# First row tiles through two PSUM tiles, earlier Sqrt table, other order of the first loads

## The chip, the cores and the metric

The kernel runs on one core of one Trainium2 chip. The metric is the device time of one execution in microseconds (us); lower is better.

PE is the matmul engine, PEld its weight loads, DVE is VectorE, ACT is ScalarE, POOL is GpSimd, SP is SyncE; ACTq and SPq are DMA issues on those engines' queues. Times in a trace count from the start of its span.

## The reference

An attention branch over 2048 rows of width 640 (32 heads of 192, the last 512 keys), a gated hidden layer (SwiGLU), and a gate that joins them. What matters here is the start of the second:

```
xn = (x - mean(x)) / sqrt(var(x) + 1e-5)          # per row, x: 2048 x 640
B  = (silu(xn @ w_gate) * (xn @ w_up)) @ w_down   # w_gate, w_up: 640 x 1536
out = x + attention(xn) * silu(B)
```

## The kernel before

The hidden layer is computed first, in four blocks of 512 rows. The first block can't wait for everything to be loaded, so it is cut into four row tiles of 128 rows. Each is normalised (statistics on DVE, the root on ACT, the scaling on DVE), transposed on PE in five chunks of 128 columns into PSUM, copied to SBUF (`xnT`), and multiplied with the first 384 columns of both weight matrices. A weight chunk is the 128 rows of a matrix that meet one of the five chunks of `xnT`; gate and up chunks are those of w_gate and w_up. Chunk-major order takes chunk by chunk over all six sums, bank-major order sum by sum over all five chunks. These make three pairs of hidden columns, f = 0, 1, 2, for which six PSUM banks stay open over the four tiles. After that come f = 3 to 11 with 512 rows at a time.

```python
        load_x(0)
        load_x(1, nc.scalar)
        for cs in (slice(0, 1), slice(1, 3), slice(3, NC)):      # weight chunks 0, 1-2, 3-4
            if cs.stop == NC:
                load_x(2)
            for eng, w_sb, w in ((nc.sync, wg_sb, B_w_gate), (nc.scalar, wu_sb, B_w_up)):
                ...
                eng.dma_start(out=w_sb[:, cs, 0:FQ], in_=src)
        load_x(3)
        ...
        nc.scalar.activation(act_t[:], one_t[:], ACT.Sqrt)       # brings in the table
        warm = sc_tile()
        keep_warm(11)                                            # dummy matmuls
        ...
        def ready(t):
            ln_transpose(t)                                      # five, all into one PSUM tile
            rows = slice(t * P, (t + 1) * P)
            n = NC if t else 2
            nc.scalar.copy(xnT[:, 0:n, rows], tps[t][:, 0:n, :])
            if n < NC:
                nc.vector.tensor_copy(out=xnT[:, n:NC, rows], in_=tps[t][:, n:NC, :])

        ln_stats(0)
        ln_sqrt(0)
        ln_stats(1, lambda: ln_apply(0, (slice(0, 2 * P), slice(2 * P, D))))
        ready(0)
        ln_sqrt(1)
        keep_warm(3)
        ...
        for t in range(4):
            order = [(*fs, [c]) for c in range(NC) for fs in banks]     # chunk-major
            if t:
                order = [(*fs, range(NC)) for fs in banks]              # bank-major
            for k, (f, s, cs) in enumerate(order):
                if k == len(order) * 3 // 5 and t < 3:
                    if t == 1:
                        ln_stats(3, lambda: ln_apply(2))
                    else:
                        ln_apply(t + 1)
                    ready(t + 1)
                    ...
                hidden_mm(first[f][s][:, rows], s, f, rows, cs)
        ...
        for b in range(NB):
            for f in range(NF):
                ...
                if b or f >= 3:
                    ffn_hidden(b, f)          # 10 matmuls, then Silu on ACT and the product on DVE
                if nx and 1 <= f < 5:
                    ln_stats(4 * b + 3 + f)   # statistics of the next block's rows, on DVE
```

The softmax here doesn't subtract the row's maximum and nothing guards it: scores larger than these inputs give would overflow.

## Time and profile before

| | before |
|---|---|
| time, median of 3 runs | 925.96 us (925.85 to 926.03) |
| span of the trace | 924.2 us |
| PE busy | 916.6 us |
| first real matmul | 7.01 us |
| transposes of row tiles 0, 1, 2, 3 start | 5.90, 8.53, 10.63, 12.75 us |
| first 512-column matmul (f = 3) | 15.65 us |
| f = 6 starts | 22.13 us |

The prediction below shows the page, the busy times by stretch and the start of the timeline. One more view also belongs here, which it did not look at: DVE after the row tiles, with the Silu table load on ACT before it and the start of f = 6 on PE (timeline; start, length, engine, line, operation, and in brackets the idle time before and what ended it).

### The profile page before, as it was taken

How to read it: one execution, taken by the hardware profiler on the slowest of the kernel's cores; microseconds unless marked ns; L12 is line 12 of the kernel's file. 1: busy time of each engine (PE TensorE's matmuls, PEld its weight loads, DVE VectorE, ACT ScalarE, POOL GpSimd, SP SyncE). 2: the span in 40 equal slices, each digit the busy share in tenths (PEclk: the TensorE clock that was granted, in tenths of full speed). 3: DMA queues.
4: the chain of work that ended last, by engine and by line, in shares of the span. 5: the costliest groups of instructions: out<-in, count | busy, mean ns of one | idle time of the engine just before them, and what ended most of it. 6: DMA issues, size and time to landing. Idle time of an engine off the chain costs nothing.

```text
span 924.2 us, 25783 instructions
## 1 busy us (share of the span) xinstructions
PE 916.6 (99%) x11101; PEld 622.6 (67%) x11101; DVE 576.1 (62%) x844; ACT 473.8 (51%) x847; POOL 100.1 (11%) x387
## 2 busy tenths in 40 slices
PE   9999999999999999999999999999999999999997
PEld 5455555575858585868686767676767777776665
DVE  6433331467676767676666667676767676767655
ACT  4222223546464656555556465655555555656561
POOL 0000000000000000000000000000000000002977
PEclk9999999999999999999999999999999999999999
DMA  9321510044544443444636252635371717162624
GB/s 297 74 54 35 114 35 1 1 81 86 83 83 80 86 80 86 72 94 66 100 59 107 57 109 53 112 50 116 45 121 40 126 37 129 35 132 74 145 47 140
DMA packets 243810, 77.18 MB, mean 84 GB/s; under 512 B 224624, under 2 KB 243696, under 8 KB 243696
## 3 DMA queue, kind: packets, MB, share of 16 engines
q1 hardware_dynamic: 242640, 74.72, 40.7%
q8 instruction: 87, 1.43, 0.7%
q10 hardware_dynamic: 1056, 0.82, 0.3%
q14 instruction: 27, 0.22, 0.1%
HBM read 39.45 MB, written 2.62 MB: 46 GB/s over the span
## 4 chain that ended last, share of the span: by engine, by line
PE 98%; DMA 1%; DVE 1%; ACTq 0%; issue 0%; ACT 0%; DVEq 0%
PE mm L430 22%; PE sc L565 19%; PE sc L444 18%; PE mm L470 16%; PE sc L276 11%; PE mm L298 6%; PE sc L539 3%; PE mm L522 2%; PE mm L539 1%; DMA wu_sb<-in_B_w_up_dram 1%; PE mm L276 0%; PE mm L311 0%; PE sc L522 0%; PE sc L470 0%; PE mm L444 0%
## 5 line engine op out<-in xcount | busy, mean ns | idle before, releaser
L448 ACT ACTIVATE p_t<-sc 128x1024 bf16<-128x1024 f32 x254 | 253.0, 1022 | 128.9 <-PE sc L444 128.9
L435 DVE TENSOR_REDUCE qT<-mm 128x512 bf16<-128x1024 f32 x189 | 230.9, 1223 | 91.6 <-PE mm L430 89.2
L500 ACT ACTIVATE O_b<-mm,r 128x192 bf16<-128x192 f32 x486 | 164.6, 421 | 183.6 <-issue 162.4
L430 PE MATMUL mm<-xnT,wq_p 64*128 64x512 bf16 x1890 | 240.0, 376 | 0.0
L590 DVE TENSOR_TENSOR sacc<-sacc,sc 128x640 f32<-128x640 f32 x200 | 164.2, 821 | 89.5 <-PE sc L565 89.5
L565 PE MATMUL sc<-wo_p,OT_b 64*128 64x320 bf16 x2592 | 217.0, 296 | 0.0
L444 PE MATMUL sc<-qT,khat 64*128 64x512 bf16 x1524 | 198.1, 376 | 0.5 <-DVE sacc L588 0.5
L470 PE MATMUL mm<-V_p,p_t 64*128 64x193 bf16 x3520 | 186.2, 242 | 0.1
L470 PEld LDWEIGHTS <-p_t 64*128 64x128 bf16 x3584 | 162.4, 93 | 12.9 <-issue 0.6
L430 PEld LDWEIGHTS <-wq_p 64*128 64x128 bf16 x1890 | 104.7, 94 | 95.7 <-issue 0.5
L565 PEld LDWEIGHTS <-OT_b 64*128 64x128 bf16 x2592 | 139.4, 94 | 22.2
L444 PEld LDWEIGHTS <-khat 64*128 64x128 bf16 x1536 | 85.1, 94 | 80.1 <-issue 0.7
L553 POOL MEMSET turn_t<- 128x1 f32 x328 | 32.2, 98 | 697.0 <-PE mm L470 474.6
L284 DVE TENSOR_TENSOR hT<-sc,sg 128x512 bf16<-128x512 f32 x46 | 31.7, 690 | 85.2 <-ACT sg L283 85.1
L283 ACT ACTIVATE sg<-sc 128x512 bf16<-128x512 f32 x46 | 27.3, 596 | 72.4 <-PE sc L276 72.4
L276 PE MATMUL sc<-xnT,wu_sb 128*128 128x512 bf16 (+1 forms) x260 | 59.1, 354 | 0.2 <-DMA wu_sb<-in_B_w_up_dram 0.2
L276 PE MATMUL sc<-xnT,wg_sb 128*128 128x512 bf16 (+1 forms) x260 | 59.2, 354 | 0.1
L298 PE MATMUL mm<-wd_sb,hT 128*128 128x320 bf16 x384 | 56.6, 299 | 0.0
L489 DVE RECIPROCAL r<-mm 128x4 f32<-128x4 f32 x124 | 22.7, 183 | 47.8 <-PE mm L470 36.3
L298 PEld LDWEIGHTS <-hT 128*128 128x128 bf16 x384 | 37.6, 98 | 18.9
L276 PEld LDWEIGHTS <-wu_sb 128*128 128x128 bf16 x285 | 26.3, 98 | 27.2 <-DMA wu_sb<-in_B_w_up_dram 0.4
L276 PEld LDWEIGHTS <-wg_sb 128*128 128x128 bf16 x285 | 26.4, 98 | 23.1 <-issue 0.2
(68 smaller groups left out, 372.9 us busy)
## 6 DMA issues: line engine op xcount, KB each, us to landing
wo_p<-in_A_wo_dram SPq DMA_DIRECT2D x16, 480.0 KB, 4.2
K_p<-in_A_k_cache_dram SPq DMA_DIRECT2D x32, 192.0 KB, 3.3
V_p<-in_A_v_cache_dram SPq DMA_DIRECT2D x32, 192.0 KB, 3.1
wq_p<-in_A_wq_dram SPq DMA_DIRECT2D x64, 80.0 KB, 3.2
wq_p<-in_A_wq_dram SPq DMA_DIRECT2D x16, 160.0 KB, 3.4
x_r<-in_A_x_dram SPq DMA_DIRECT2D x16, 160.0 KB, 3.9
x_t<-in_A_x_dram SPq DMA_DIRECT2D x14, 160.0 KB, 3.0
OT_b<-O_b SPq DMA_TRANSPOSE x124, 2.8
```

The source lines that it names most:

```text
L276: nc.tensor.matmul(out, w_sb[:, c, f * P : (f + 1) * P], xnT[:, c, qc], start=(c == 0), stop=(c == NC - 1),)
L298: nc.tensor.matmul(dn[:, 0:HD], hTs[b][:, f, ti * P : (ti + 1) * P], wd_sb[:, f, cols], start=(f == 0), stop=(f == NF - 1),)
L430: nc.tensor.matmul(q_ps[:, h, :], pairs[pr]["wq"][r, c, j * P : (j + 1) * P], xnT[r, c, b * 512 : (b + 1) * 512], start=(c == 0), stop=(c ...
L435: nc.vector.reduce_sum(qTs[i][:, j, :], q_ps[:, :, :].rearrange("p h n -> p n h"), axis=AX.X)
L444: nc.tensor.matmul(sc[:, h, :], khat[r, j, ks], qT[r, j, :], start=(j == 0), stop=(j == 2))
L448: nc.scalar.activation(p_t[:, :, :], sc[:, :, :], ACT.Exp, scale=scale)
L470: m = nc.tensor.matmul(acc[:, k, h * 256 : h * 256 + Dh + 1], Ps[i][kc][r, h, qt * P : (qt + 1) * P], V_p[r, kc, h, 0 : Dh + 1], start=(p ...
L500: nc.scalar.activation(O_b[:, qt, h, :], a_k[:, h, 0:Dh], ACT.Copy, scale=r[:, k, h, :])
L539: nc.tensor.matmul(ps, OTs[i][:, 3 * qt + j, :], pairs[i // NB]["wo"][:, j, n * HD : (n + 1) * HD], start=(first and j == 0), stop=(end an ...
L553: st["turn"] = nc.gpsimd.memset(turn_t[:], 0.0)
L565: m = nc.tensor.matmul(ps[:, n, 0:HD], OTs[i][r, 3 * qt + j, :], pairs[i // NB]["wo"][r, j, n * HD : (n + 1) * HD], start=(turn == 0 and j ...
L590: nc.vector.tensor_tensor(s_t, s_t, sc[:, :, 0:HD], ALU.add)
```

## The change

It means to bring the first real matmuls forward: the Sqrt table is loaded while the first transfers run, the first two chunks of a row tile go to a PSUM tile of their own so that their copy need not wait for all five transposes, ACT makes both copies, and x tile 2 goes behind weight chunk 3. Tiles 1 and 2 run chunk-major to suit this. The PSUM banks of the start belong to a pool that is closed after f = 3.

```diff
@@ loads
-        for cs in (slice(0, 1), slice(1, 3), slice(3, NC)):
-            if cs.stop == NC:
-                load_x(2)
-            for eng, w_sb, w in ((nc.sync, wg_sb, B_w_gate), (nc.scalar, wu_sb, B_w_up)):
-                ...
+        load_first(slice(0, 1), (nc.sync, nc.sync))       # gate on the first engine, up on the second
+        load_first(slice(1, 3), (nc.sync, nc.sync))
+        nc.scalar.activation(act_t[:], one_t[:], ACT.Sqrt)
+        load_first(slice(3, 4), (nc.sync, nc.scalar))
+        load_x(2)
+        load_first(slice(4, NC), (nc.sync, nc.scalar))
         load_x(3)
@@ PSUM, dummies
-        nc.scalar.activation(act_t[:], one_t[:], ACT.Sqrt)
-        keep_warm(11)
+        PARTS = (slice(0, 2), slice(2, NC))
+        tps = [psum1.tile([P, 8, P], bf, name="tp", tag="tp%d" % n) for n in range(2)]
+        ...
+        keep_warm(9)
+        keep_warm(6, P)
@@ ready(t)
-            n = NC if t else 2
-            nc.scalar.copy(xnT[:, 0:n, rows], tps[t][:, 0:n, :])
-            if n < NC:
-                nc.vector.tensor_copy(out=xnT[:, n:NC, rows], in_=tps[t][:, n:NC, :])
+            for tp, cs in zip(tps, PARTS):
+                for k, c in enumerate(range(cs.start, cs.stop)):
+                    nc.tensor.transpose(tp[:, k, :], xn[:, c * P : (c + 1) * P], ident[:])
+            for tp, cs in zip(tps, PARTS):
+                nc.scalar.copy(xnT[:, cs, rows], tp[:, 0 : cs.stop - cs.start, :])
@@ row tiles
-        keep_warm(3)
-            if t:
+            if t == 3:
                 order = [(*fs, range(NC)) for fs in banks]
@@ after the row tiles
+        ffn_hidden(0, 3, [psum1.tile([P, 512], f32, name="gu3", tag="tp%d" % n)[:, :] for n in range(2)])
+        early.close()
+        mm_pool.append(...)
-                if b or f >= 3:
+                if b or f >= 4:
                     ffn_hidden(b, f)
```

More of the change, by code (lines that the diff above doesn't have):

```diff
@@ L68 @@
     qpool = ctx.enter_context(tc.tile_pool(name="att_q", bufs=2))
-    psum = ctx.enter_context(tc.tile_pool(name="psum", bufs=2, space=bass.MemoryType.PSUM))
+    sc_pool = ctx.enter_context(tc.tile_pool(name="psum_sc", bufs=2, space=bass.MemoryType.PSUM))
+    mm_pool = []
     def sc_tile():
-        return psum.tile([P, 2, 512], f32, name="sc", tag="sc")
+        return sc_pool.tile([P, 2, 512], f32, name="sc")
     def mm_tile():
-        return psum.tile([P, 2, 512], f32, name="mm", tag="mm")
+        return mm_pool[0].tile([P, 2, 512], f32, name="mm")
     ctx.enter_context(tc.manual_schedule())
@@ L181, in load_x, with load_first @@
             x_t[t] = lnx.tile([P, D], bf, name="x_t")
-            if t == 0:
-                for r, eng in ((lo, nc.sync), (hi, nc.scalar)):
-                    eng.dma_start(out=x_t[t][r, :], in_=x2[t * P + r.start : t * P + r.stop, :])
-            else:
-                eng.dma_start(out=x_t[t][:], in_=x2[t * P : (t + 1) * P, :])
+            for r, eng in ((lo, nc.sync), (hi, nc.scalar)) if t == 0 else ((slice(0, P), eng),):
+                eng.dma_start(out=x_t[t][r, :], in_=x2[t * P + r.start : t * P + r.stop, :])
+        def load_first(cs, engs):
+            for eng, w_sb, w in zip(engs, (wg_sb, wu_sb), (B_w_gate, B_w_up)):
+                src = w[cs.start * P : cs.stop * P, 0:FQ].rearrange("(c p) f -> p c f", p=P)
+                eng.dma_start(out=w_sb[:, cs, 0:FQ], in_=src)
         def load_gu(q):
@@ L198 @@
         load_x(1, nc.scalar)
-        for cs in (slice(0, 1), slice(1, 3), slice(3, NC)):
-            if cs.stop == NC:
-                load_x(2)
-            for eng, w_sb, w in ((nc.sync, wg_sb, B_w_gate), (nc.scalar, wu_sb, B_w_up)):
-                src = w[cs.start * P : cs.stop * P, 0:FQ].rearrange("(c p) f -> p c f", p=P)
-                eng.dma_start(out=w_sb[:, cs, 0:FQ], in_=src)
+        load_first(slice(0, 1), (nc.sync, nc.sync))
[4 more added lines that the diff above has]
+        load_first(slice(4, NC), (nc.sync, nc.scalar))
         load_x(3)
@@ L211, with keep_warm @@
         nc.sync.dma_start(out=wd_sb[:], in_=B_w_down.rearrange("(f p) d -> p f d", p=P))
-        nc.scalar.activation(act_t[:], one_t[:], ACT.Sqrt)
-        warm = sc_tile()
-        def keep_warm(n):
-            for _ in range(n):
-                nc.tensor.matmul(warm[:, 0, :], zero_t[:, 0:P], zero_t[:], start=True, stop=True)
-        keep_warm(11)
+        early = ExitStack()
+        psum1 = early.enter_context(tc.tile_pool(name="psum1", bufs=1, space=bass.MemoryType.PSUM))
+        PARTS = (slice(0, 2), slice(2, NC))
+        tps = [psum1.tile([P, 8, P], bf, name="tp", tag="tp%d" % n) for n in range(2)]
+        first = [
+            [gu[:, s, :] for s in range(2)]
+            for gu in (sc_tile(), sc_tile(), psum1.tile([P, 2, 512], f32, name="gu"))
+        ]
+        def keep_warm(n, cols=512):
+            for _ in range(n):
+                nc.tensor.matmul(
+                    first[2][1][:, 0:cols], zero_t[:, 0:P], zero_t[:, 0:cols], start=True, stop=True
+                )
+        keep_warm(9)
+        keep_warm(6, P)
         def ln_stats(t, between=None):
@@ L256, in ln_apply @@
                 )
-        tps = {}
-        def ln_transpose(t):
-            xn = xns.pop(t)
-            tps[t] = tp[:, t % 2, 0 : NC * P].rearrange("p (c k) -> p c k", c=NC)
-            for c in range(NC):
-                nc.tensor.transpose(tps[t][:, c, :], xn[:, c * P : (c + 1) * P], ident[:])
         def ln_transpose_dma(t):
@@ L284, in hidden_gate, with ffn_hidden @@
             nc.vector.tensor_tensor(hTs[b][:, f, :], u, sg[:], ALU.mult)
-        def ffn_hidden(b, f):
-            gu = mm_tile() if (b, f) == (0, 3) else sc_tile()
+        def ffn_hidden(b, f, gu=None):
+            gu = gu or [sc[:, s, :] for sc in (sc_tile(),) for s in range(2)]
             for s in range(2):
-                hidden_mm(gu[:, s, :], s, f, slice(b * 512, (b + 1) * 512))
-            hidden_gate(b, f, gu[:, 0, :], gu[:, 1, :])
+                hidden_mm(gu[s], s, f, slice(b * 512, (b + 1) * 512))
+            hidden_gate(b, f, *gu)
         def ffn_down(b, u):
@@ L317 @@
         hTs[0] = ffh.tile([P, NF, 512], bf, name="hT")
-        first = {f: [sc[:, s, :] for s in range(2)] for f, sc in ((0, sc_tile()), (1, sc_tile()))}
-        tp = psum.tile([P, 2, 1024], bf, name="tp", tag="mm")
-        first[2] = [mm[:, s, :] for mm in (mm_tile(),) for s in range(2)]
         def ready(t):
-            ln_transpose(t)
-            rows = slice(t * P, (t + 1) * P)
-            n = NC if t else 2
-            nc.scalar.copy(xnT[:, 0:n, rows], tps[t][:, 0:n, :])
-            if n < NC:
-                nc.vector.tensor_copy(out=xnT[:, n:NC, rows], in_=tps[t][:, n:NC, :])
+            xn, rows = xns.pop(t), slice(t * P, (t + 1) * P)
+            for tp, cs in zip(tps, PARTS):
[3 more added lines that the diff above has]
+                nc.scalar.copy(xnT[:, cs, rows], tp[:, 0 : cs.stop - cs.start, :])
         ln_stats(0)
@@ L359 @@
                     hidden_gate(0, f, *first[f])
+        ffn_hidden(0, 3, [psum1.tile([P, 512], f32, name="gu3", tag="tp%d" % n)[:, :] for n in range(2)])
+        early.close()
+        mm_pool.append(ctx.enter_context(tc.tile_pool(name="psum_mm", bufs=2, space=bass.MemoryType.PSUM)))
         nc.gpsimd.memset(V_p[:, :, :, Dh : Dh + 2], 1.0)
```

## The prediction

> **What bounds the kernel now.** I read the page first: its busy shares, its digits in 40 slices and its chain of waits.
>
> ```profile
> PE 916.6 (99%) x11101; PEld 622.6 (67%) x11101; DVE 576.1 (62%) x844; ACT 473.8 (51%) x847; POOL 100.1 (11%) x387
> ...
> DMA  9321510044544443444636252635371717162624
> ...
> PE 98%; DMA 1%; DVE 1%; ACTq 0%; issue 0%; ACT 0%; DVEq 0%
> ```
>
> The matmul engine is the bound: of the 924.2 us span it is busy 916.6, and the chain that ended last runs 98% through it. Only 7.6 us are left in which it does nothing. The transfers show 9 in the first slice alone. So I asked for busy time by stretch, to see where those 7.6 us lie (columns: stretch, length, busy us of PE, PEld, DVE, ACT, POOL with counts, clock, DMA share, GB/s).
>
> ```profile
> 0.00:15.60 15.60, 13.56 (x154) 9.62 (x155) 7.42 (x25) 6.34 (x13) 0.79 (x8) 1.00 0.89 273
> 15.60:176.00 160.40, 160.40 (x925) 86.55 (x924) 56.68 (x109) 49.31 (x89) 3.81 (x6) 1.00 0.26 61
> 176.00:185.00 9.00, 9.00 (x86) 4.09 (x84) 6.92 (x8) 6.03 (x6) 0.00 (x0) 1.00 0.01 2
> 185.00:895.00 710.00, 709.37 (x9750) 503.99 (x9745) 487.54 (x678) 406.56 (x724) 75.98 (x360) 1.00 0.44 83
> 895.00:924.20 29.20, 24.28 (x199) 18.39 (x196) 17.50 (x27) 5.53 (x16) 19.56 (x13) 0.98 0.49 136
> ```
>
> From 15.6 to 895 us PE is full, less 0.6 us. The change touches nothing after about 17 us: with line and buffer numbers left out, the two programs' instruction orders are the same from there on, except that one set of PSUM banks is handed over earlier. So what it can win is what it takes off the start, before PE becomes full. Every us by which the 4 row tiles of the first block finish sooner should reach the end, because nothing later waits for anything but PE.
>
> The timeline of that start (start, length, engine, line, operation, and in brackets the idle time before it and its releaser):
>
> ```profile
> 3.57 0.89 DVE L229 BATCH_NORM_STATS2 stats<-x_t 128x6 f32<-128x320 bf16 x2 [2.40 <-DMA x_t<-in_A_x_dram]
> 3.58 1.28 ACT L214 ACT_TABLE_LOAD   x1 [3.58 <-DMA x_t<-in_A_x_dram]
> ...
> 4.87 0.20 ACT L214 ACTIVATE act_t<-one_t 128x1 f32<-128x1 f32 x1
> ...
> 4.98 0.28 ACT L242 ACTIVATE rstd<-mv,eps_t 128x1 f32<-128x1 f32 x1
> ...
> 6.56 0.37 ACT L327 COPY xnT<-tp 128x256 bf16<-128x256 bf16 x1 [1.30 <-PE tp L264]
> ...
> 6.97 0.36 DVE L329 COPY xnT<-tp 128x384 bf16<-128x384 bf16 x1 [0.19 <-ACT xnT L327]
> ...
> 7.91 0.23 PE L276 MATMUL sc<-xnT,wu_sb 128*128 128x128 bf16 x1 [0.24 <-DMA wu_sb<-in_B_w_up_dram]
> ...
> 9.31 0.49 DVE L229 BATCH_NORM_STATS2 stats<-x_t 128x6 f32<-128x320 bf16 x1 [0.40 <-DMA x_t<-in_A_x_dram]
> ```
>
> The reader should see three kinds of wait: a table load stuck behind a DMA issue, so the first Sqrt starts at 4.98 although its statistics end at 4.70; a copy at 6.56 that waits for all five transposes, and a second that waits for the first; and two transfers that are themselves late, the weight chunk at 7.91 and x tile 3 at 9.31.
>
> **What the Trainium skill says.** "ScalarE: Activation LUTs", section "What ACT_TABLE_LOAD costs", gives about 1283 ns for a load plus about 1380 ns for a drain. The trace has 1.28 us for the load, with the next activation right behind it, so I count 1.28 us, no drain. "PSUM — Partial Sum Buffer", section "PSUM bank collisions raise a hardware error", says accesses of two engines must be kept apart by bank and quadrant, two readers included. The trace agrees: the DVE copy starts 0.03 us after the ACT copy of the same bank ends. "DMA: Bandwidth & Descriptors", section "Issuing engines are not separate DMA queues", says that spreading issues over engines saves only issue time. The trace fits: both queues together move 330 to 350 GB/s from 5.4 us on. "TensorE: Matmul & The Clock Gate", section "What's actually happening", puts the cold array at half clock until a busy window has passed; here the dummy matmuls go from 427 ns apart to 216 at 4.61 us.
>
> **The change part by part.**
>
> *Table load.* ACT now does it after two issues, about 1.9 to 3.4 us, hidden. The statistics end at 4.70; the Sqrt can start near 4.74 instead of 4.98. The reciprocal then waits for the statistics half in front of it (4.62 + 0.44 = 5.06) and starts near 5.09 instead of 5.29: **0.20 us** off the chain to the first transpose, 5.90 to about 5.69. The 9 + 6 dummy matmuls fit before it: they end near 5.2 if the clock rises at 4.61 again.
>
> *Two PSUM tiles.* The first copy waits only for two transposes. In the trace the second transpose starts at 5.96 and takes 0.22, against 6.54 for the last: some 0.33 us earlier. It starts near 6.02, ends near 6.39, and PE's first real matmul comes at 6.44 instead of 7.01. The same trace has a further 0.11 us hole at 7.12 to 7.23, where the third real matmul waits for the dummies that wrote its tile; the dummies now write another tile. So the first chunk's six matmuls end **0.65 to 0.7 us** earlier, at about 6.78.
>
> *Both copies on ScalarE.* A copy costs 0.372 us for 256 columns and 0.692 for 640, thus 0.83 ns a column; 384 cost about 0.48. Both, overlapping by 0.09, take 0.76 in place of 0.69: later row tiles get their last chunks 0.1 later but their first two some 0.25 sooner, which suits the new chunk-major order of tiles 1 and 2. DVE is spared 0.36 us once.
>
> *Chunk-major order.* In tiles 1 and 2, 12 matmuls instead of 15 follow the next tile's transposes: 12 x 56 ns = 0.67 us instead of 0.84. PE then stood 0.16 to 0.26 us at the head of each of tiles 1 to 3 for the five-chunk copy. Together about 0.2 us a tile, if the next tile is ready.
>
> *Transfers.* All arrive at the same saturated engines. Before, up chunk 1-2 (ACT queue) landed at 7.86 while gate chunk 1-2 had landed at 6.95, x tile 2 at 7.70, last weights at 8.64 and 8.82, x tile 3 at 9.29. Ahead of the second weight chunk there are now about 0.92 MB and no x tile 2 (0.16 MB), which at 330 GB/s is 0.5 us: I estimate it at 7.0 to 7.3. x tile 2 slides by perhaps 0.3 us to 8.0; x tile 3 has the same 1.64 MB through it, so 8.8 to 9.3.
>
> *The sum.* Now go along the row tiles. Tile 0 starts at 6.44, runs dry at 6.78 and waits for the second weight chunk to about 7.1; tile 1's transposes come near 7.85 instead of 8.53, tile 1 starts near 8.9 instead of 9.76, 0.8 us ahead. Then tile 2 meets the transfers. In DVE's order the statistics of x tile 3 come before tile 2 is normalised, so tile 2's transposes come no earlier than x tile 3's landing plus 1.25 us (0.49 + 0.16 + 0.45 and the gaps between), or x tile 2's plus 2.35. With 9.1 and 8.0 that is 10.35, against 10.63. Of the 0.8 us only about 0.3 survives there. Tile 3's transposes follow 2.1 us later, as before (2.12), because that distance is a chain of DVE and ACT and not of PE; then the 0.15 to 0.2 us of the order comes on top. End of the block: 0.3 + 0.15, about **0.45 us** sooner, and the rest of the kernel moves along with it. 925.96 - 0.45 = 925.5.
>
> **The rivals.** *First: the transfers take it all.* If x tile 3 lands at 9.3 or later again, tile 2 is not earlier, and only the shorter tail of each tile is left: 0.15 to 0.2 us, time 925.8. For it: the DMA engines were at their ceiling and the bytes are the same; x tile 2 even goes later, and issuing x tile 3 now has to wait for an up chunk to land. Against: the following large weight transfer is also issued later and competes less with it. *Second: the transfers get better than I think.* With fewer descriptors in front, both x tiles could land 0.5 us earlier; then the 0.8 us of tile 1 survives: 925.1. *Third: ScalarE becomes the bound of the start.* It carries two copies, Sqrt and two issues per tile; but 0.76 + 0.30 in a period of 2.1 us leaves half of it free. *Fourth: the hidden start.* If the clock of the array rises later than 4.61 us, 15 shorter dummies with no later refill leave it cold at the first tile: 30 matmuls at 107 ns instead of 56 would cost up to 1.5 us. The trace shows full clock from 4.61, so I give this little. *Fifth: the new PSUM layout or handover delays the second block.* Its banks are free long before; nothing.
>
> **Range and chances.** Three runs of before differ by 0.2 us, so the noise is small; the size of the gain is the doubt. From no gain (first rival with a bit of bad luck) to 1.0 us (second) gives 924.95 to 925.95. Over 2% would be 18.5 us; the whole start with idle PE is 2 us, so 2% faster can't happen, and 2% slower would take a fault I don't see.
>
> **What would show each step.** Right: the table load at about 2 us and the first Sqrt near 4.75; first transpose near 5.7; first copy near 6.0, while later transposes still run; first real matmul near 6.45; a wait for a weight chunk until about 7.1; first 512-column matmul after the row tiles near 15.2 instead of 15.65; after that equal durations and no new wait. Wrong: the first real matmul not before 6.8; tile 2's transposes at 10.6 or later, or before 10.0; the weight chunk later than 7.5; or a gain at the start that is gone again at the end.

## More of the kernel before

From f = 4 on, two PSUM tiles take turns for the hidden columns (f = 3 has another one): f = 6 writes the tile that f = 4 used, and may only do so when DVE has formed f = 4's product.

```profile
13.95 1.28 ACT L356 ACT_TABLE_LOAD   x1
...
15.96 1.29 DVE L284 TENSOR_TENSOR hT<-sc,sg 128x512 bf16<-128x512 f32 x2 [3.27 <-ACT sg L283]
17.16 0.68 DVE L284 TENSOR_TENSOR hT<-mm,sg 128x512 bf16<-128x512 f32 x1
17.76 0.88 DVE L229 BATCH_NORM_STATS2 stats<-x_t 128x6 f32<-128x320 bf16 x2
...
19.79 0.64 DVE L284 TENSOR_TENSOR hT<-mm,sg 128x512 bf16<-128x512 f32 x1
20.35 0.88 DVE L229 BATCH_NORM_STATS2 stats<-x_t 128x6 f32<-128x320 bf16 x2
...
21.38 0.64 DVE L284 TENSOR_TENSOR hT<-sc,sg 128x512 bf16<-128x512 f32 x1
...
22.13 1.24 PE L276 MATMUL sc<-xnT,wg_sb 128*128 128x512 bf16 x5
```

From its first product at 15.96 DVE has no waiting row in this stretch: the bracket stands only on the first. It does products and statistics back to back, and f = 4's product (the last DVE row) ends at 22.02. PE takes up f = 6 at 22.13. In the changed kernel PE follows such a product by 0.055 us when it really waits for it, so PE could have started at 22.08 here. It came 0.05 us later than it was allowed to. No wait is shown, and there is almost no room either.

## The result, and the profile after

The changed kernel takes 925.76 us (median of 6 runs, 925.57 to 925.99), the kernel before 925.90 us in 6 runs (925.52 to 926.17). The ratio is 0.9999 with a 95% interval of 0.9986 to 1.0011: the same. A ratio here is the mean time of one kernel's fast runs over that of the other's of the same rounds, so it is not quite the ratio of the medians.

| | before | changed | predicted |
|---|---|---|---|
| first transpose | 5.90 | 5.63 | 5.69 |
| first real matmul | 7.01 | 6.37 | 6.44 |
| second gate chunk / up chunk lands | 6.95 / 7.86 | 7.31 / 7.71 | - / 7.0 to 7.3 |
| x tile 2 / x tile 3 lands | 7.70 / 9.29 | 8.43 / 9.07 | 8.0 / 8.8 to 9.3 |
| transposes of tile 1 | 8.53 | 8.38 | 7.85 |
| transposes of tile 2 | 10.63 | 10.64 | 10.35 |
| first 512-column matmul | 15.65 | 15.34 | 15.2 |
| f = 6 starts | 22.13 | 22.09 | with the lead of the row before |

A landing is the start of an issue plus the time to landing that the trace gives for it. The page's busy shares and chain of the changed kernel:

```profile
PE 916.3 (99%) x11102; PEld 627.2 (68%) x11102; DVE 575.8 (62%) x843; ACT 474.4 (51%) x851; POOL 100.1 (11%) x387
...
PE 97%; DVE 1%; DMA 0%; SPq 0%; issue 0%; DVEq 0%
```

Nothing has moved that a page could show. The timeline of the start answers to the rows in the prediction:

```profile
1.94 1.28 ACT L204 ACT_TABLE_LOAD   x1 [1.94 <-issue]
2.00 0.38 ACTq L189 DMA_DIRECT2D wu_sb<-in_B_w_up_dram  x1
...
4.70 0.29 ACT L254 ACTIVATE rstd<-mv,eps_t 128x1 f32<-128x1 f32 x1 [1.26 <-DVE mv L244]
...
5.95 0.82 ACT L331 COPY xnT<-tp 128x256 bf16<-128x256 bf16 x2 [0.96 <-PE tp L329]
...
7.35 0.23 PE L280 MATMUL sc<-xnT,wg_sb 128*128 128x128 bf16 x1 [0.48 <-DMA wg_sb<-in_B_w_gate_dram]
...
7.76 0.23 PE L280 MATMUL sc<-xnT,wu_sb 128*128 128x128 bf16 x1 [0.18 <-DMA wu_sb<-in_B_w_up_dram]
...
8.45 0.89 DVE L241 BATCH_NORM_STATS2 stats<-x_t 128x6 f32<-128x320 bf16 x2 [0.81 <-DMA x_t<-in_A_x_dram]
```

The Sqrt now waits for its statistics and not for the table, and the copies start at 5.95 instead of 6.56. But after six real matmuls PE stands still for the gate chunk and then for the up chunk, and DVE for x tile 2. Where before one matmul waited 0.24 us for a weight chunk, now two wait, 0.66 us in all. The second row shows something else: the issue of up chunk 3 goes out at 2.00 while the table load runs (1.94 to 3.22).

And ACT, DVE and PE after the row tiles, in the same timeline:

```profile
13.74 1.28 ACT L357 ACT_TABLE_LOAD   x1
...
15.76 1.29 DVE L288 TENSOR_TENSOR hT<-sc,sg 128x512 bf16<-128x512 f32 x2 [3.17 <-ACT sg L287]
...
16.96 1.50 DVE L288 TENSOR_TENSOR hT<-gu,sg 128x512 bf16<-128x512 f32 x2
...
18.38 0.88 DVE L241 BATCH_NORM_STATS2 stats<-x_t 128x6 f32<-128x320 bf16 x2
...
21.39 0.64 DVE L288 TENSOR_TENSOR hT<-sc,sg 128x512 bf16<-128x512 f32 x1
...
22.09 1.24 PE L280 MATMUL sc<-xnT,wg_sb 128*128 128x512 bf16 x5
```

DVE's first product starts 0.20 us earlier than before, yet f = 4's product (last DVE row) starts at 21.39 as it did before at 21.38. The second DVE row tells why: two products take 1.50 us, where two back to back take 1.29 (the DVE row above it). There is a hole of 0.12 us in it; f = 3's product, now ahead of the statistics, has to wait for f = 3's matmuls. PE, which started f = 3 at 15.34 and needs 30 matmuls of 216 ns to get to f = 6, is there at 21.82 and starts at 22.09. It waits 0.27 us (the row has no bracket: PE's last matmul is counted as busy to 21.98, and the 0.11 us that are left are too short to be marked), and the lead of 0.31 us over the kernel before shrinks to 0.04. At the first Exp of the attention (170.26 us before, 170.22 changed) it is still 0.04. Also, DVE's own lead is 0.20 us and not 0.31 from the start: its first product waits for the first Silu, and the Silu table load stands on ACT behind the copies of the last row tile, from 13.74 us here and from 13.95 before.

So there are three questions. What holds tile 2 at the same time in both kernels? What makes the stretch from there to the 512-column matmul 0.3 us shorter (5.02 us before, 4.69 changed)? And is it DVE that takes it back?

### The profile page after: what moved, and what is told of

It reads as the page before. It is cut to its first block, busy times and chain, and to the rows that moved or that the text cites. A ratio compares the mean times of both kernels' runs of the same rounds, so it can differ in the third digit from the quotient of the medians.

```text
span 924.0 us, 25790 instructions
## 1 busy us (share of the span) xinstructions
PE 916.3 (99%) x11102; PEld 627.2 (68%) x11102; DVE 575.8 (62%) x843; ACT 474.4 (51%) x851; POOL 100.1 (11%) x387
## 4 chain that ended last, share of the span: by engine, by line
PE 97%; DVE 1%; DMA 0%; SPq 0%; issue 0%; DVEq 0%
PE mm L434 22%; PE sc L569 19%; PE sc L448 18%; PE mm L474 16%; PE sc L280 10%; PE mm L302 6%; PE sc L543 3%; PE mm L526 2%; PE mm L543 1%; DMA x_t<-in_A_x_dram 0%; DVE stats L241 0%; PE gu L280 0%; PE mm L315 0%; PE sc L474 0%; PE sc L526 0%; SPq L189 0%
```

## The experiments

Twelve kernels ran in three sets, each set on one chip beside new runs of the kernel before. The landings move from run to run, so the traces are compared by differences: from the up chunk 1-2's landing to tile 1's transposes, from there or from an x tile's landing to tile 2's transposes (T2), from T2 to the first 512-column matmul, and from that to f = 6.

| trace | up chunk lands | tile 1 | x tile 2, 3 land | T2 | T2 to 512 | 512 to f = 6 | f = 6 |
|---|---|---|---|---|---|---|---|
| before | 7.86 | 8.53 | 7.70, 9.29 | 10.63 | 5.02 | 6.47 | 22.13 |
| before_again | 7.45 | 8.13 | 7.97, 9.40 | 10.52 | 5.02 | 6.47 | 22.01 |
| loads_only | 7.28 | 7.97 | 8.26, 8.92 | 10.47 | 5.02 | 6.47 | 21.96 |
| changed | 7.71 | 8.38 | 8.43, 9.07 | 10.64 | 4.69 | 6.75 | 22.09 |
| after_again | 7.51 | 8.19 | 8.22, 8.89 | 10.44 | 4.69 | 6.75 | 21.88 |
| psum_only | 8.14 | 8.81 | 8.70, 10.08 | 11.35 | 4.68 | 6.75 | 22.79 |
| table_late | 7.40 | 8.07 | 8.10, 9.63 | 10.75 | 4.69 | 6.75 | 22.19 |
| gate_in_loop | 7.88 | 8.55 | 8.54, 9.37 | 10.76 | 4.69 | 6.54 | 21.99 |
| x2_early | 7.91 | 8.59 | 8.34, 9.42 | 10.58 | 4.69 | 6.54 | 21.81 |
| stats_later | 7.99 | 8.66 | 8.68, 9.36 | 10.90 | 4.69 | 6.48 | 22.06 |
| one_psum | 7.45 | 8.12 | 8.14, 10.08 | 11.20 | 5.02 | 6.75 | 22.97 |
| no_x23 | 7.64 | 8.31 | not loaded | 10.30 | 4.69 | 6.75 | 21.74 |
| no_w12_x23 | not loaded | 8.00 | not loaded | 10.04 | 4.69 | 6.75 | 21.48 |
| both | 7.75 | 8.42 | 8.19, 9.11 | 10.41 | 4.69 | 6.47 | 21.57 |

The times of the sets:

| run | median (lowest to highest), us | before beside it | ratio, 95% interval |
|---|---|---|---|
| psum_only | 926.17 (925.74 to 926.65) | 926.07 (925.60 to 926.44) | 1.0001, 0.9988 to 1.0013 |
| loads_only | 925.93 (925.65 to 926.01) | the same | 0.9997, 0.9985 to 1.0010 |
| gate_in_loop | 925.62 (925.55 to 926.01) | the same | 0.9996, 0.9982 to 1.0009 |
| stats_later | 928.19 (927.76 to 929.44) | the same | 1.0024, 1.0012 to 1.0037 |
| before_again | 925.86 (925.76 to 926.30) | 925.73 (925.59 to 925.99) | 1.0003, 0.9990 to 1.0017 |
| after_again | 925.64 (925.45 to 926.08) | the same | 1.0000, 0.9988 to 1.0013 |
| table_late | 925.86 (925.57 to 926.17) | the same | 1.0001, 0.9989 to 1.0014 |
| x2_early | 925.43 (925.42 to 926.54) | the same | 1.0000, 0.9987 to 1.0012 |
| no_x23 | 925.62 (925.18 to 925.76) | 925.91 (925.52 to 926.15) | 0.9997, 0.9985 to 1.0010 |
| no_w12_x23 | 925.02 (924.90 to 925.21) | the same | 0.9991, 0.9977 to 1.0004 |
| one_psum | 926.12 (925.92 to 926.60) | the same | 1.0004, 0.9992 to 1.0017 |
| both | 925.22 (925.05 to 925.35) | the same | 0.9994, 0.9981 to 1.0006 |

All count as the same at 2%; of the intervals only that of stats_later leaves 1 out. What follows rests on the traces.

### psum_only and loads_only: the two halves apart

psum_only is the changed kernel with the old issue order and the old place of the Sqrt; loads_only is the kernel before with the new ones.

```diff
 psum_only (against the changed kernel)
-        load_first(slice(0, 1), (nc.sync, nc.sync)) ... load_first(slice(4, NC), ...)
+        for cs in (slice(0, 1), slice(1, 3), slice(3, NC)): ...   # as before
+        nc.scalar.activation(act_t[:], one_t[:], ACT.Sqrt)         # after all loads, as before
 loads_only (against the kernel before): the same hunk the other way
```

> The changed kernel with the issue order of the loads and the place of the Sqrt table load put back to those of the kernel before: two PSUM tiles, both copies on ScalarE, chunk-major order and the other dummies stay. Theory T (the lead of the row tiles is lost when the seventh pair of hidden columns, f = 6, has to wait for a PSUM tile that VectorE frees): first real matmul near 6.65 us, tile 2's transposes near 10.55, first 512-column matmul near 15.3 (before 15.65, changed 15.34), f = 6 again at 22.05 to 22.1, whole time 0.0 to 0.1 us under before. Rival R (the loads decide the whole effect): first 512-column matmul at 15.65 again, and time equal to before.

> The kernel before with the new issue order of the loads and the early Sqrt table alone; one PSUM tile, DVE's second copy, bank-major tiles stay. Theory T: first real matmul near 6.8 us, second weight chunks landing at 7.3 and 7.7 as in the changed kernel, x tile 2 at 8.4, so tile 2's transposes near 10.65 and first 512-column matmul at 15.6 to 15.7; time within 0.1 us of before. Rival R: first 512-column matmul near 15.35 as in the changed kernel.

The absolute expectations missed, both of them. psum_only's 512-column matmul came at 16.04 us and not at 15.3, because in this execution its transfers landed late (gate chunk 1-2 at 7.96, x tile 3 at 10.08), although they are issued as in the kernel before; loads_only's came at 15.49 and not at 15.65. One trace cannot tell 0.3 us of such a thing, which I had not reckoned with. The differences told it all the same. From T2 on, psum_only takes 4.68 us and loads_only 5.02: the 0.33 us belong to the PSUM and order part, and none of it to the loads. psum_only also has the 6.75 us from there to f = 6, loads_only the old 6.47.

### before_again and after_again: how much the landings move

Both kernels unchanged, traced a second time.

> The kernel before, unchanged, traced a second time, to see how far the landings move from run to run. In the six traces so far the transposes of row tile 2 start at the later of x tile 2's landing plus 2.2 us and x tile 3's plus 1.25 to 1.35; expected here: x tile 3's landing plus 1.3, whatever it is, the first 512-column matmul 5.02 us after those transposes, and no wait at f = 6. If the landings were fixed by the program, x tile 3 would land at 9.3 again; if the memory's rate varies, anywhere from 8.8 to 10.1.

> The changed kernel, unchanged, traced a second time. Expected: tile 2's transposes at x tile 2's landing plus 2.2, the first 512-column matmul 4.7 us after them (0.33 less than in the kernel before), f = 6 starting 6.75 us after that one instead of 6.48, so 0.27 of the 0.33 given back. Time 0.05 to 0.15 us under before if the landings are alike.

The kernel before: up chunk at 7.45 instead of 7.86, x tile 2 at 7.97 instead of 7.70. The changed kernel: x tile 2 at 8.22 instead of 8.43. The expectation of before_again that tile 2 comes 1.3 us after x tile 3's landing missed: it was 1.12. The later differences repeat to 0.01 us (5.02 and 6.47; 4.69 and 6.75). T2, where the transfers meet the chain, is 10.63 and 10.52 in one kernel, 10.64 and 10.44 in the other: no difference that the loads could be credited with. From T2 to f = 6 it is 11.50 us before and 11.44 changed: **0.05 us** is what the change brings in both pairs of traces.

### What sets tile 2

In every row of the table with a loaded up chunk, tile 1's transposes start 0.67 to 0.69 us after that chunk lands: 11 matmuls at 56 ns have to run between. It is so with the first real matmul at 7.01 and with it at 6.35. T2 then is the latest of these: tile 1 plus 2.0 us (1.99 to 2.04, and 2.1 in the kernel before; a chain of copies, Sqrt, reciprocal and scaling), x tile 2's landing plus 2.22, x tile 3's landing plus 1.12. Tile 1 sets it in before, x2_early and no_x23 (in "both" tile 1 and x tile 2 give the same), x tile 2 in the changed kernel, after_again, loads_only, gate_in_loop and stats_later, x tile 3 in before_again, table_late and one_psum. psum_only has a fourth: PE waits at 9.67 for the gate's chunk 3-4, and gets to tile 2 after it.

To test this as a cause, two kernels leave transfers out. Their results are wrong (the comparison with the reference passed all the same).

```diff
 no_x23
         def load_x(t, eng=nc.sync):
+            if t in (2, 3):
+                x_t[t] = x_t[t - 2]
+                return
 no_w12_x23, in addition
-        load_first(slice(1, 3), (nc.sync, nc.sync))
-                    out, w_sb[:, c, ...], xnT[:, c, qc],
+                    out, w_sb[:, 0 if f < 3 and c in (1, 2) else c, ...], xnT[:, c, qc],
```

> Wrong result on purpose: the changed kernel without the loads of x tiles 2 and 3, whose rows are taken from tiles 0 and 1 that are there. In ten traces tile 1's transposes start 0.67 us after the up chunk 1-2 lands, and tile 2's at the latest of three: tile 1's plus 2.0, x tile 2's landing plus 2.2, x tile 3's plus 1.1 to 1.3. Expected by that rule: tile 2's transposes at tile 1's plus 2.0, that is 2.67 us behind the up chunk (10.2 to 10.6), first 512-column matmul 4.69 later, time 0.1 to 0.3 us under the changed kernel. Rival (the x tiles alone hold the start): tile 2's transposes near 9.9.

> Wrong result on purpose: as no_x23, and weight chunks 1 and 2 of the first columns are not loaded either (chunk 0 is used for them), so neither of the transfers named waits. By the rule tile 1 is then set by its own normalisation (ends near 7.65): tile 1's transposes near 7.7, tile 2's near 9.75, first 512-column matmul near 14.45, f = 6 near 21.2, time 0.8 to 0.9 us under the changed kernel: what the shorter chain at the start would be worth if the data were there. Rival: another transfer or engine holds the tiles, tile 2's transposes later than 10.1.

no_x23 did what the rule says: tile 1 0.67 us after the up chunk (7.64 to 8.31), T2 1.99 us after tile 1, at 10.30. The rival's 9.9 did not come. The PE rows of no_x23:

```profile
7.06 0.23 PE L283 MATMUL sc<-xnT,wg_sb 128*128 128x128 bf16 x1 [0.21 <-DMA wg_sb<-in_B_w_gate_dram]
7.68 0.23 PE L283 MATMUL sc<-xnT,wu_sb 128*128 128x128 bf16 x1 [0.39 <-DMA wu_sb<-in_B_w_up_dram]
8.31 0.44 PE L332 MATMUL tp<-ident,xn 128*128 128x128 bf16 x5
10.30 0.45 PE L332 MATMUL tp<-ident,xn 128*128 128x128 bf16 x5
```

PE still waits twice for weights, and nothing stands before the transposes but their own chain. With those chunks gone as well, tile 1 came at 8.00 and T2 at 10.04. I had put them at 7.7 and 9.75; one half of x tile 0 landed at 3.73 instead of 3.43 in this execution, and everything behind it is 0.3 us later, first transposes at 5.92 instead of 5.63. Tile 1 is now set by its own normalisation, and so no earlier than the 7.97 of loads_only. Even so this is the earliest T2 of all (0.40 to 0.60 us before those of the two kernels traced twice) and the fastest kernel, 0.9 us under before. So the transfers do hold the start, and with the data there the changed kernel is faster (924.90 to 925.21 us, all under its lowest run with them, 925.45). How much of that is the shorter chain at the start is not shown: the same loads were not taken out of the kernel before. With the loads in place, the first real matmul comes 0.64 us sooner and T2 does not.

### table_late: the Sqrt behind the issues again

```diff
-        nc.scalar.activation(act_t[:], one_t[:], ACT.Sqrt)
         load_first(slice(3, 4), (nc.sync, nc.scalar))
         ...
+        nc.scalar.activation(act_t[:], one_t[:], ACT.Sqrt)         # after the last load
```

> The changed kernel with the Sqrt table load put back behind ScalarE's DMA issues. Theory (the second weight chunk and x tile 2 hold the row tiles, not the first transposes): first transposes 0.2 us later, near 5.85, first real matmul near 6.6, but the seventh to twelfth real matmul, tile 2's transposes and the time as in the changed kernel. Rival (each 0.1 us off the chain before the first transposes reaches the end): tile 2's transposes and the time 0.2 us later.

This edit did not do what it was meant to do. ACT has two weight loads to issue here and three in the kernel before. The second went out at 2.41 us (2.42 before), so the table load ran at 2.90 to 4.18 and was still in time; the first transposes were not later (5.60). In the kernel before it is the third issue that goes out only at 3.16, just after a half of x tile 0 has landed at 3.14, and it pushes the table load to 3.58. So no run shows what the earlier table load is worth alone. And with the earliest first real matmul of all (6.35), T2 was a late one (10.75), x tile 3 having landed at 9.63.

### one_psum: one PSUM tile, two copies

```diff
-        tps = [psum1.tile([P, 8, P], bf, name="tp", tag="tp%d" % n) for n in range(2)]
+        one = psum1.tile([P, 8, P], bf, name="tp", tag="tp0")
+        tps = [one[:, cs, :] for cs in PARTS]
```

> The changed kernel with the five transposes of a row tile in one PSUM tile again, still two copies on ScalarE. Theory A (the second PSUM tile shortens the chain of every tile): first real matmul 0.9 to 1.05 us after the first transpose instead of 0.74, tile 1's transposes still 0.67 us after the up chunk, and first 512-column matmul 4.9 to 5.0 us after tile 2's transposes. Theory B (the chunk-major order and the 12 matmuls in the tail do it): 4.69 as in the changed kernel.

Theory A holds, with the first and the last number just beyond the ranges named. The first real matmul comes 1.08 us after the first transpose (5.68 to 6.76) instead of 0.74, and from T2 to the 512-column matmul it is 5.02 us again: without the second PSUM tile all of the 0.33 us is gone. The chunk-major order and the two copies on ACT alone bring nothing there; whether the second tile would bring it all without the chunk-major order was not run. ACT's rows of this run show the first copy at 6.34, after the last transpose, where the changed kernel had it at 5.95:

```profile
6.34 0.76 ACT L332 COPY xnT<-tp 128x256 bf16<-128x256 bf16 x2 [1.30 <-PE tp L330]
```

### gate_in_loop and stats_later: who takes the lead back

gate_in_loop emits f = 3 in the loop again, so DVE does its product behind the statistics of x tiles 4 and 5 as in the kernel before. stats_later moves the statistics and scaling of the second block two pairs of columns later.

```diff
 gate_in_loop
-        ffn_hidden(0, 3, [...]); early.close(); mm_pool.append(...)
         for b in range(NB): for f in range(NF):
-                if b or f >= 4:
+                if (b, f) == (0, 3):
+                    ffn_hidden(0, 3, [...]); early.close(); mm_pool.append(...)
+                elif b or f >= 4:
 stats_later
+                d = 2 if b == 0 else 0
-                if nx and 1 <= f < 5:
-                    ln_stats(4 * b + 3 + f)
+                if nx and 1 <= f - d < 5:
+                    ln_stats(4 * b + 3 + f - d)       # ln_apply and its transposing DMA likewise
```

> The changed kernel with the fourth pair of hidden columns (f = 3) emitted in the loop again, behind the statistics of x tiles 4 and 5, as in the kernel before; nothing else. Theory T: VectorE runs without a hole from its first gate product, frees the PSUM tile 0.2 us sooner, so f = 6 starts at 21.85 to 21.9 instead of 22.09, and the time is 0.2 us under the changed kernel (925.5 to 925.6). Rival: the lead is lost to something else (DMA, or a later wait), f = 6 stays at 22.09 or the 0.2 us are gone again by 170 us, time 925.75.

> The changed kernel with the statistics and normalisation of the second block (x tiles 4 to 7) moved two pairs of hidden columns later, so that VectorE is free for the gate product of f = 4. Theory T: no wait at f = 6, which starts at 21.82 (first 512-column matmul at 15.34 plus 30 times 216 ns), and the lead of 0.3 us over the kernel before reaches the end: time 0.25 us under the changed kernel, 925.5. Rival: a later wait takes it, time 925.75.

Both confirm DVE by the differences; the starts of f = 6 themselves (21.99 and 22.06 us) missed the expected ones, because T2 was late in both traces. gate_in_loop has no hole (its f = 4 product starts 5.43 us after its first, as before with 5.42; changed 5.64), and the 6.75 us become 6.54:

```profile
17.08 0.68 DVE L288 TENSOR_TENSOR hT<-gu,sg 128x512 bf16<-128x512 f32 x1
17.68 0.88 DVE L241 BATCH_NORM_STATS2 stats<-x_t 128x6 f32<-128x320 bf16 x2
...
21.30 0.64 DVE L288 TENSOR_TENSOR hT<-sc,sg 128x512 bf16<-128x512 f32 x1
```

So of the 0.27 us that the changed kernel waits at f = 6, 0.21 come from its own new order on DVE. The other 0.06 to 0.07 stay with the old order: PE is 0.31 us earlier, DVE only 0.20, and there were 0.05 to spare. stats_later has 6.48, that is 30 matmuls of 216 ns with no wait at all. But its mean time is 2.3 us longer than that of the kernel before, because the same statistics have a second deadline: the second block needs its transposed rows, and now PE waited for them:

```profile
37.52 1.24 PE L280 MATMUL sc<-xnT,wg_sb 128*128 128x512 bf16 x5 [2.34 <-DMA xnT<-xn]
```

My expectation had not looked for that. DVE's stretch is tied at both ends: too much in front delays f = 6, too much behind delays the second block.

### x2_early and both: a version from what was learnt

x2_early is gate_in_loop with x tile 2 issued before weight chunk 3. "both" is the changed kernel with x tile 2 there, and with only the statistics of x tile 6 moved, from f = 3 to behind the product of f = 4; those of tile 7 and the scaling stay where they were.

```diff
 x2_early and both
         load_first(slice(1, 3), (nc.sync, nc.sync))
+        load_x(2)
         ...
         load_first(slice(3, 4), (nc.sync, nc.scalar))
-        load_x(2)
 both
-                    ln_stats(4 * b + 3 + f)
+                    for g in ({3: (), 4: (3, 4)}.get(f, (f,)) if b == 0 else (f,)):
+                        ln_stats(4 * b + 3 + g)
```

> The kernel of the run gate_in_loop with x tile 2 issued ahead of weight chunk 3, not behind it. Theory (x tile 2's late landing sets tile 2): x tile 2 lands 0.3 to 0.5 us sooner, tile 2's transposes come at its landing plus 2.2 or x tile 3's plus 1.25, 10.3 to 10.4, first 512-column matmul near 15.05, time 0.3 us under gate_in_loop. Rival (weight chunk 3 then lands too late and the matmuls of tile 0 wait instead): tile 1's transposes or the six matmuls behind them wait, tile 2's transposes not before 10.7.

> The changed kernel with the statistics of x tile 6 put behind the gate product of f = 4 on VectorE, and x tile 2 issued ahead of weight chunk 3. Expected: no wait at f = 6, which starts 6.47 us after the first 512-column matmul instead of 6.75, no new wait at f = 7 or at the second block; tile 2's transposes by the rule of three landings, 10.4 to 10.6. Time 0.3 us under the changed kernel and 0.35 to 0.4 under before. Rival: f = 7 or the second block waits instead and the 0.27 us do not arrive.

x tile 2 landed at 8.34 and 8.19, against 8.10 to 8.68 where it is issued behind chunk 3: 0.5 us earlier in the queue is not seen in the landing beyond the noise, and whether that place is better stays open. The expectation of x2_early missed: T2 came at 10.58 and not at 10.3 to 10.4, set by tile 1. The move of the statistics works. In "both" the product of f = 4 is done before the statistics of x tile 6, and PE starts f = 6 at 21.57 with no wait:

```profile
20.04 0.21 DVE L244 BATCH_NORM_AGGREGATE mv<-stats 128x2 f32<-128x12 f32 x1
20.25 0.69 DVE L288 TENSOR_TENSOR hT<-sc,sg 128x512 bf16<-128x512 f32 x1
20.85 0.88 DVE L241 BATCH_NORM_STATS2 stats<-x_t 128x6 f32<-128x320 bf16 x2
```

No new wait shows at f = 7 or at the second block, and its first Exp comes at 169.71 us, 0.55 us before that of the first trace of before and 0.44 before that of the second. Its five runs, 925.05 to 925.35 us, all lie under the lowest of the nine of before beside them, 925.52. The interval of the ratio still holds 1, so this is a good sign for a version that beats both, not a proof. The time was 0.69 us under before by the medians, more than the 0.35 to 0.4 expected. Of the 0.55 us, 0.33 is the stretch shortened by the second PSUM tile, which now arrives, and 0.22 is T2, in which the luck of the landings is included.

## Why the prediction was right or wrong

**The time and the class: right.** 925.76 us lies in the stated range, and nothing near 2% happened. The gain was put at 0.45 us; the medians give 0.14, and what both pairs of traces show is 0.05. So the middle was about three times too hopeful even by the medians. That the sum still lies in the range is partly luck, for errors of opposite sign met in it: 0.28 us were to be won at tile 2 and none were, 0.15 to 0.2 in the tails and it was 0.33, and nothing was to be lost after that and 0.27 were. Three of the prediction's own signs of being wrong came: tile 2's transposes after 10.6 (10.64), the weight chunk after 7.5 (7.71), a gain at the start that is gone at the end.

**Table load, two PSUM tiles: right, and hidden behind the transfers at that place.** First transposes at 5.63 (foretold 5.69), first real matmul at 6.37 (6.44). I said that the first six matmuls would end 0.65 to 0.7 us earlier and that a wait for the weights would follow. Both hold.

**Transfers: the term that was mis-sized.** I had the second up chunk at 7.0 to 7.3; it landed at 7.71 and 7.51. Tile 1 is 0.67 us behind it, so it came at 8.38 and not at 7.85. x tile 2 came at 8.43 and 8.22 and not at 8.0. One error is visible: I let ACT issue up chunk 3 only after the table load, at 3.4 us. It went out at 2.00 and was in at 4.87, long before it is used, ahead of chunks 1-2. That it delayed them is an inference from shared transfer engines; no run took it away. The other error is to have read one trace's landings as constants. They move by several tenths from one execution to the next, which is as large as the effect that I worked out from them.

**The rule for tile 2: right in form.** I said x tile 3's landing plus 1.25 or x tile 2's plus 2.35; measured are 1.12 and 2.22, and tile 1 plus 2.0, which I had not named, beside them. My first rival ("the transfers take it all", 925.8) named what happened up to there: tile 2 is no earlier, 10.63 and 10.64. But it was x tile 2 that held it, not x tile 3, which landed at 9.07 and not at 9.3 or later.

**The tail of each tile: too small, and for another reason.** I gave the order 0.15 to 0.2 us. The stretch from tile 2 to the end is 0.33 us shorter, and one_psum shows that it needs the second PSUM tile: 12 matmuls in place of 15 alone do not bring it. I had also read too much into the trace: PE stood idle 0.26 us at the head of tile 1, but 0.11 at those of tiles 2 and 3, where I had written 0.16.

**"Nothing later waits for anything but PE": the step that failed.** From a PE that is busy all the time from 15.6 us on I took it that every lead reaches the end. A busy PE shows that nobody makes it wait at its present pace; it does not show what happens if it comes earlier. Of the lead of 0.31 us, 0.27 was lost at f = 6, for two reasons. About 0.21 was the change's own doing: I had written that the instruction orders are the same after about 17 us, and they are so on PE, but DVE does f = 3's product at 17.77 us and not at 19.79, ahead of two tiles' statistics, and has to wait for it. I had looked at that move only for PE and its banks (fifth rival). The remaining 0.06 or so was the missing room: f = 6 had only 0.05 us to spare on DVE, and DVE, behind the Silu table load, came 0.20 us sooner and not 0.31.

**The others.** ScalarE did not become the bound of the row tiles. The fourth rival (a cold array) was nearer than I thought. In the trace of the changed kernel the matmuls reach full pace (55 ns apart) only at 5.35 us, not at 4.61, with the first transpose at 5.63. In that of gate_in_loop, whose start is the same, real matmuls are still 107 ns apart at 6.67 to 6.88 us. It cost nothing there, because PE waited for the weights until 7.93 anyway; that is luck of this place.

## What to carry to other kernels

Before you credit a lead on the bounding engine to the end, look at each engine that hands it buffers, measure the distance between its release and the taker, and ask whether that engine gets the same lead: where the distance is small and it does not, the lead ends there. When transfers meet a chain, write the start of each step as a landing plus a constant and check the constants over several traces; landings move from run to run, the constants here moved by no more than 0.05 us. An edit that leaves one engine's order as it was may still change another's, so compare the orders of all of them.

## What the Trainium skill lacked or had wrong

- "ScalarE: Activation LUTs", section "What ACT_TABLE_LOAD costs", gives about 2.66 us for a switch, drain included. Here the next activation starts 11 ns after a load of 1.28 us, in both kernels: no drain is seen. Nor does one stand before a load: that of Silu starts 17 ns after the copy in front of it in the kernel before.
- The same page does not say that a DMA issue on ScalarE's queue can pass during a table load. Here one that stands behind it in the program goes out at 2.00 us, with the load running from 1.94 to 3.22.
- "DMA: Bandwidth & Descriptors" gives rates and fixed costs, but no spread. With the same issue order (before, before_again, psum_only), x tile 2 landed at 7.70, 7.97 and 8.70 us and x tile 3 at 9.29, 9.40 and 10.08.
- "PSUM — Partial Sum Buffer", section "PSUM bank collisions raise a hardware error", is about correctness. What the wait costs here, no page has: one PSUM tile instead of two makes the first copy wait for all five transposes and costs 0.34 us per chain at the start (1.08 against 0.74) and 0.33 us by the end of the block.
